# First batch of a fused attention and two-layer MoE kernel: both token parts per third of the gate and value weights

## Chip, cores and metric

The kernel runs on one core of one Trainium2 chip. The metric is device time in microseconds, the median over runs. Engines are named as in the profile: PE (TensorE matmul), PEld (its weight loads), DVE (VectorE), ACT (ScalarE), POOL (GpSimd), SP (SyncE, which here only issues DMAs). ACTq and SPq are the DMA-issuing queues of ACT and SP.

## What is computed

Three stages, cut to what matters:

```python
def _attn_ref(q, k, v, p):                 # q, k, v: 8 x 8 x 576 x 64; p: 8 x 8 x 32 x 64
    p_packed = sm_attn(p, k, v)            # 32 rows per head
    return sm_attn(q, p_packed, p_packed)
def _moe_ref(x, w_gate, w_val, w_out, rms_g):   # 4608 tokens, 512 -> 1536 -> 512
    xn = x / rms * rms_g
    return silu(xn @ w_gate) * (xn @ w_val) @ w_out
def _moe2_ref(x, w_in, w_out, a, b):            # 512 -> 2048 -> 512
    h = x @ w_in
    g = P(h) / (Q(h) + 1e-6)                    # cubic over quadratic
    return g @ w_out
```

The three weights of the first MoE layer arrive as 64-bit floating-point numbers.

## The kernel before

**Batches.** The eight batches of 576 tokens run one after the other through attention and the first MoE layer; the second layer runs at the end over all tokens. A batch's tokens are cut into two parts (`PARTS`): h=0 has 256 of them and h=1 has 320. While batch b is in its MoE layer, attention of batch b+1 is worked in between. Batches 1 to 6 follow an order written out by hand (`BLOCK`). Everything before that, the first batch, is put in order per engine by the framework's list scheduler, which takes the program's order as priority and runs an instruction early where its inputs and buffers are there; the order it finds is fixed before the program runs.

**Precision.** Each matmul is a sum of three fp16 passes over a high and a low half (`PASSES`). So a chain of one output tile has 6 matmuls for the gate or value product and 36 for an output tile of `w_out`.

**Weights of the first layer.** They come in 36 pieces of 128 x 512: eight for each of three thirds `fr` (four of `w_gate`, four of `w_val`), then twelve of `w_out`. For each piece (class `Weights`) the ACT queue issues a DMA of 512 KB into one of three `raw64` buffers (L159). `decode` turns the 64-bit words into fp32 with three DVE instructions (L140, L144, L146) into one of two `raw32` buffers. `split` then makes the two fp16 halves: for gate and value pieces by two fp32 matmuls and an fp16 one on PE (L191, L194, tile `wlo`) and two ACT instructions (L192, L195); for `w_out` by ACT (L115) and DVE (L118).

**M.** The gate and value weights are multiplied with the packed rows of the batch into twelve tiles `mt` (`m_make`: 6 matmuls at L628, then ACT L282 and DVE L283), four to each third. The pool `mt` has 12 buffers. For the first batch `m_make` asks for its weights with `w1.have`, so M0 to M3 pull in the first third's pieces, M4 to M7 the second's, M8 to M11 the third's.

**Gate and value.** For each part h and each of 12 chunks c: a gate chain (L976, 6 matmuls), tanh on ACT (L987), a product on DVE (L991), a value chain (L976), a product on DVE (L994), and the two halves of y by ACT (`y_hi`, L1001) and POOL (`y_lo`, L1006). Four chunks use one third of the weights. The pool `y` has 12 buffers. PSUM has five banks under the tag `m` for all of `wlo`, M, gate, value and output tiles of the first batch.

**Output.** `out1_first` (part h=0 of the first batch) holds all four output tiles in four of those five banks and adds chunk after chunk, so that it can take each piece of `w_out` as it comes (L1042). `out1_slots` (h=1) makes one output tile after the other. `store_x2` writes them out through ACT L1011, DVE L1015 and SP's queue (L1029).

**Slots.** The first batch is cut into 72 slots by the `yield`s of these generators. After each slot `a_step` adds the pieces of attention of batch 1 that `A_PLAN_0` lists for it: `ks`/`kt`, `qs`/`qt`, `vs` are the splits (L115, L118) and transposing DMAs (L358) of k, q, v; `am`...`at` the first softmax (L379 to L436, its transposing DMA on SP); `bm`, `bs`, `bt` the packed rows (L460, L478); `cm`, `cx`, `ce`, `cn`, `ct` the second softmax in three units (matmul L495, DVE L509 to L529, transposing DMA L543); `xm`, `xq`, `xr`, `xt` the attention output and its normalisation into `an`; M0 to M11 the next batch's M. Batch 0's own attention runs before slot 0 in the order `FIRST`. In it and in the plan, `cn` puts the softmax's last product (L529) on DVE and `cN` the same on POOL.

Before the change the slots are: 0 to 23 gate and value of h=0 (the M of a third stands ahead of its first chunk), 24 to 35 `out1_first`, 36 to 59 gate and value of h=1, 60 to 71 `out1_slots` of h=1.

Of the kernel before, what the change touches and what calls it, by code (L numbers as in the profile page):

```python
# [9 lines left out]
F32 = mybir.dt.float32  # L10
F16 = mybir.dt.float16
# [26 lines left out]
def attention_pack_glu_rational_kernel(  # L38
# [22 lines left out]
    KC = DM // 128  # L61
# [213 lines left out]
    def attention(b):  # L275
# [672 lines left out]
    )  # L948

    A_PLAN_0 = (  # L950
# [8 lines left out]
    )  # L959

    FIRST = (
# [3 lines left out]
    )  # L965

# [29 lines left out]
    def y_hi(b, h, c, t):  # L996
        if (b, h) == (B - 1, 1):
            y = yl_p[0].tile([128, 2, PW], F16, name=f"yl{c}")
        else:
            y = y_p.tile([128, 2, PW], F16, tag="y", bufs=YB, name="y")[:, :, 0:t.shape[1]]  # L1000
        act(out=y[:, 0], in_=t, func=AF.Copy)  # L1001
        ys[b, h, c] = y
# [67 lines left out]
        for d in range(KC):  # L1070
            store_x2(b, h, d, pss[d])

    def gv_slots(b, h):
        for c in range(NF1):
            if b == 0 and h == 0 and c % 4 == 0:
                for i in range(c, c + 4):
                    at0[f"M{i}"]()
            ps = gv_mm("g", b, h, c)
            t = gate_tanh(ps)
            gate_mul(t, ps)  # L1080
            yield
            glu_mul(t, gv_mm("v", b, h, c))
            y_hi(b, h, c, t)
            y_lo(b, h, c, t)
            yield
# [51 lines left out]
    for t in (pkz[0], pkz[1], a16, pT):  # L1137
        nc.gpsimd.memset(t, 0.0)
    nc.gpsimd.memset(m_half, -0.5)
    ident = y_p.tile([128, 2, PW], F16, tag="y", bufs=YB, name="ident")  # L1140
    ident = ident.rearrange("p a t -> p (a t)").bitcast(F32)[:, 0:128]
    make_identity(nc, ident)
    nc.gpsimd.dma_start(out=g_raw, in_=rms_g.rearrange("(k p) -> p k", p=128))
    nc.gpsimd.dma_start(out=ab[:, 0:4], in_=pa.rearrange("(o n) -> o n", o=1).to_broadcast([128, 4]))
    nc.gpsimd.dma_start(out=ab[:, 4:6], in_=pb.rearrange("(o n) -> o n", o=1).to_broadcast([128, 2]))
    SH = S_X2 * S_WI2

    def squares(n, name):
        t = y_p.tile([128, 2, PW], F16, tag="y", bufs=YB, name=name).rearrange("p a t -> p (a t)")
        return [t.bitcast(F32)[:, 128 * i:128 * i + 128] for i in range(n)], t[:, 256 * n:256 * n + 128]  # L1150


    diag, minus = squares(2, "diag01")
    diag = diag + squares(2, "diag23")[0]

    def constants():
        nc.vector.tensor_scalar_mul(g_sc, g_raw, S_WGV)
# [20 lines left out]
    def a_step(b, slot):  # L1178
        if b not in plan:
            plan[b] = attention(b + 1)  # L1180
        for at, names in A_PLAN_0:
            if at == slot:
                for nm in names.split():
                    plan[b][nm]()
# [55 lines left out]
            nc.sync.dma_start(out=t, in_=w2_dram[it[:3]])  # L1240

    slot = 0
    for h in range(2):
        for g in (gv_slots(0, h), out1_slots(0, h) if h else out1_first(0, h)):
            for _ in g:
                a_step(0, slot)
                slot += 1
    an.pop(0)
    w2.start()

# [219 lines left out]
```

## Time and profile before

| | us |
|---|---|
| median of 3 runs | 1639.94 (1639.42 to 1644.54) |
| profiled execution, its own time | 1638.45 |
| span in its trace | 1636.3 |
| PE busy | 1538.1 (94%) |
| DVE busy | 1308.2 (80%) |
| first batch ends (PE starts batch 1) | 228.4 after the span's start |

The page gives, among others, the busy share of each engine in 40 equal slices of the span (40.9 us each), the chain of waits that ended last, and groups of instructions. The views by window give busy microseconds of each engine in a stretch, with the granted clock of TensorE as a share of full speed. A group of instructions has its count, busy time, the mean of one in ns, and after the bar the engine's idle time just before them and what ended it.

### The profile page before, as it was taken

How to read it: one execution, taken by the hardware profiler on the slowest of the kernel's cores; microseconds unless marked ns; L12 is line 12 of the kernel's file. 1: busy time of each engine (PE TensorE's matmuls, PEld its weight loads, DVE VectorE, ACT ScalarE, POOL GpSimd, SP SyncE). 2: the span in 40 equal slices, each digit the busy share in tenths (PEclk: the TensorE clock that was granted, in tenths of full speed). 3: DMA queues.
4: the chain of work that ended last, by engine and by line, in shares of the span. 5: the costliest groups of instructions: out<-in, count | busy, mean ns of one | idle time of the engine just before them, and what ended most of it. 6: DMA issues, size and time to landing. Idle time of an engine off the chain costs nothing.

```text
span 1636.3 us, 27117 instructions
## 1 busy us (share of the span) xinstructions
PE 1538.1 (94%) x10158; PEld 901.9 (55%) x10158; DVE 1308.2 (80%) x2201; ACT 937.2 (57%) x1881; POOL 540.5 (33%) x638
## 2 busy tenths in 40 slices
PE   4876899999999998999999999999999999999998
PEld 2424577676767677676776444444444444444443
DVE  5878858678786767867559998989898989898980
ACT  4654547565575655656457756656565656565650
POOL 1200224143342413424233433433343433343430
PEclk9898999999999999999999999999999999999999
DMA  8668427476574746636450101010101010100000
GB/s 204 177 184 201 117 64 191 110 164 145 127 190 93 178 102 149 150 89 139 122 185 15 39 1 52 1 52 1 52 0 52 1 52 1 52 1 26 1 26 26
DMA packets 230899, 144.44 MB, mean 88 GB/s; under 512 B 172272, under 2 KB 208112, under 8 KB 229616
## 3 DMA queue, kind: packets, MB, share of 16 engines
q1 hardware_dynamic: 195600, 91.59, 24.0%
q10 hardware_dynamic: 35072, 51.13, 10.5%
q8 instruction: 79, 1.29, 0.3%
q14 instruction: 52, 0.43, 0.1%
q0 software_dynamic: 96, 0.01, 0.0%
HBM read 82.32 MB, written 27.26 MB: 67 GB/s over the span
## 4 chain that ended last, share of the span: by engine, by line
PE 71%; DVE 16%; DMA 5%; ACT 4%; issue 3%; POOL 1%; ACTq 0%; SPq 0%; DVEq 0%; POOLq 0%
PE h L1315 22%; PE o L1386 21%; PE o L1042 11%; PE gv L976 10%; DVE raw L144 2%; PE mm L856 2%; DVE t L994 2%; DVE t L991 2%; PE xo L814 1%; DVE raw L140 1%; DVE raw L146 1%; PE mm L628 1%; DVE v L699 1%; DMA aT<-a 1%; DMA kT<-x16in 1%
## 5 line engine op out<-in xcount | busy, mean ns | idle before, releaser
L1386 PE MATMUL o<-w2o,g 128*128 128x512 f16 x1728 | 397.3, 380 | 7.1 <-DVE osb L1380 3.8
L1315 PE MATMUL h<-xi,w2i 128*128 128x512 f16 x1728 | 396.3, 379 | 0.0
L976 PE MATMUL gv<-an,mt 128*128 128x256 f16 (+1 forms) x2304 | 302.3, 287 | 19.0 <-DVE t L991 14.3
L1386 PEld LDWEIGHTS <-g 128*128 128x128 f16 x1728 | 169.2, 98 | 214.3 <-issue 7.9
L1042 PE MATMUL o<-y,wo 128*128 128x256 f16 (+1 forms) x2160 | 277.9, 287 | 6.5 <-POOL y L1006 3.2
L1315 PEld LDWEIGHTS <-w2i 128*128 128x128 f16 x1728 | 169.1, 98 | 200.9
L976 PEld LDWEIGHTS <-mt 128*128 128x128 f16 x2304 | 221.2, 98 | 95.3 <-issue 40.0
L1042 PEld LDWEIGHTS <-wo 128*128 128x128 f16 x2304 | 223.3, 98 | 74.1 <-issue 10.2
L1006 POOL TENSOR_TENSOR y<-t,y 128x256 f16<-128x256 f32 (+1 forms) x180 | 139.2, 776 | 315.2 <-ACT y L1001 312.3
L1330 POOL TENSOR_SCALAR w<-ah,cf 128x512 f32<-128x512 f32 x144 | 111.3, 773 | 373.8 <-DVE t L1347 156.4
L1353 POOL TENSOR_TENSOR g<-t,g 128x512 f16<-128x512 f32 x144 | 173.9, 1208 | 99.4 <-issue 71.4
L1327 ACT ACTIVATE ah<-h 128x512 f32<-128x512 f32 x144 | 85.6, 594 | 206.5 <-PE h L1315 206.2
L1345 DVE SCALAR_TENSOR_TENSOR w<-w,r 128x512 f32<-128x512 f32 x144 | 178.8, 1241 | 4.0 <-ACT r L1344 4.0
L1335 DVE TENSOR_TENSOR w<-w,ah 128x512 f32<-128x512 f32 x144 | 135.9, 944 | 0.0
L1333 DVE TENSOR_TENSOR t<-t,h 128x512 f32<-128x512 f32 x144 | 98.3, 683 | 42.6 <-ACT t L1328 42.1
L1328 ACT ACTIVATE t<-h,cf 128x512 f32<-128x512 f32 x144 | 111.5, 774 | 22.8 <-POOL g L1353 22.6
L1015 DVE SCALAR_TENSOR_TENSOR x2e<-o,x2e 128x256 f16<-128x256 f32 (+1 forms) x64 | 29.0, 454 | 106.0 <-ACT x2e L1011 105.9
L1334 DVE SCALAR_TENSOR_TENSOR t<-t,cf,h 128x512 f32<-128x512 f32 x144 | 107.7, 748 | 5.1
L1346 DVE SCALAR_TENSOR_TENSOR t<-t,cf,r 128x512 f32<-128x512 f32 x144 | 107.3, 745 | 0.0
L1001 ACT ACTIVATE y<-t 128x256 f16<-128x256 f32 (+1 forms) x180 | 77.6, 436 | 51.9 <-DVE t L994 51.1
L1347 DVE SCALAR_TENSOR_TENSOR t<-w,t 128x512 f32<-128x512 f32 x144 | 99.6, 692 | 4.9
L1343 ACT ACTIVATE r<-w,one 128x512 f32<-128x512 f32 x144 | 103.5, 719 | 0.0
(192 smaller groups left out, 1795.3 us busy)
## 6 DMA issues: line engine op xcount, KB each, us to landing
raw<-in_moe_w_out_dram ACTq DMA_DIRECT2D x28, 512.0 KB, 4.4
xi<-x2s SPq DMA_DIRECT2D x9, 1024.0 KB, 5.7
raw<-in_v_dram SPq DMA_DIRECT2D x16, 512.0 KB, 4.7
raw<-in_q_dram SPq DMA_DIRECT2D x16, 512.0 KB, 4.9
raw<-in_moe_w_in_dram ACTq DMA_DIRECT2D x16, 512.0 KB, 4.7
out_dram<-osb SPq DMA_DIRECT2D x32, 256.0 KB, 2.5
raw<-in_k_dram SPq DMA_DIRECT2D x14, 512.0 KB, 4.9
raw<-in_moe_w_gate_dram ACTq DMA_DIRECT2D x12, 512.0 KB, 3.8
```

What stands on the lines that cost most here:

```text
L976: nc.tensor.matmul(out=ps, lhsT=mt[b, nm, c // 4, g][:, l, cs], rhs=an[b][:, 2 * r_ + g, cols], start=(n == 0), stop=(n == 5))
L1006: nc.gpsimd.tensor_tensor(out=y[:, 1], in0=t, in1=y[:, 0], op=ALU.subtract)
L1042: nc.tensor.matmul(out=ps, lhsT=wo1[c][:, l, d * 128:(d + 1) * 128], rhs=ys[b, h, c][:, r_, :], start=(c == 0 and n == 0), stop=(c == NF1 ...
L1315: nc.tensor.matmul(out=ps, lhsT=w[:, l, cs], rhs=x2in[j][:, r_, kc, :], start=(n == 0), stop=(n == 3 * KC - 1))
L1328: act(out=t, in_=ps, func=AF.Identity, scale=cf[:, 0:1], bias=cf[:, 7:8])
L1330: nc.gpsimd.tensor_scalar(out=w, in0=ah, scalar1=cf[:, 6:7], scalar2=cf[:, 5:6], op0=ALU.mult, op1=ALU.add)
L1334: stt(out=t, in0=t, scalar=cf[:, 1:2], in1=ps, op0=ALU.add, op1=ALU.mult)
L1335: nc.vector.tensor_tensor(out=w, in0=w, in1=ah, op=ALU.mult)
L1345: stt(out=w, in0=w, scalar=Q1, in1=r0, op0=ALU.add, op1=ALU.mult)
L1346: stt(out=t, in0=t, scalar=cf[:, 2:3], in1=r0, op0=ALU.add, op1=ALU.mult)
L1353: nc.gpsimd.tensor_tensor(out=g[:, 1], in0=t, in1=g[:, 0], op=ALU.subtract)
L1386: nc.tensor.matmul(out=ps, lhsT=gs[j, c][:, l, t * 128:(t + 1) * 128], rhs=w2t["o", 0, c][:, r_, :], start=(c == 0 and n == 0), stop=(c == ...
```

## The change

The first batch no longer finishes part h=0 before it turns to h=1. It takes gate and value of h=0 and then of h=1 with the first third, the same with the second third, then h=0 with the last third, `out1_first` of h=0, h=1 with the last third, and `out1_slots` of h=1:

| slots | before | after |
|---|---|---|
| 0 to 7 | h=0, first third | h=0, first third |
| 8 to 15 | h=0, second third | h=1, first third |
| 16 to 23 | h=0, last third | h=0, second third |
| 24 to 31 | `out1_first` (24 to 35) | h=1, second third |
| 32 to 39 | h=1, first third (36 to 43) | h=0, last third |
| 40 to 51 | h=1, second and last third (44 to 59) | `out1_first` |
| 52 to 59 | | h=1, last third |
| 60 to 71 | `out1_slots`, h=1 | `out1_slots`, h=1 |

With it come four smaller edits. The plan of attention of batch 1 is spread anew: the first softmax and q's split move from slots 11 to 25 and 27 to 30 to slots 16 to 33 and 27 to 31, the packed rows from 25 and 32 to 33 and 37, the second softmax from 34 to 50 to 40 to 51, the attention output from 47 to 61 to 50 to 61, and M0 to M11, which were spread over slots 44 to 63, stand in 60 to 71. `cN` becomes `cn` for unit 0 of batch 0 and unit 2 of batch 1. The y of h=0, chunks 4 to 11, goes into buffers of the pool `mt`. The identity and diagonal matrices go into a buffer of the pool `an` instead of three of the pool `y`.

```diff
     A_PLAN_0 = (
-        (0, "L pl ps"), (2, "ks0 vs0"), (4, "kt0 L"), (6, "pp L"), (8, "ks1 kt1"),
-        (11, "L am0 ax0"), (14, "ae0 as0"),
-        (17, "an0 at0"), (20, "am1 ax1"), (23, "ae1 as1"), (25, "bm0 bs0 bt0 an1 at1"), (26, "vs1"),
-        (27, "L qs0 qt0"), (29, "L"), (30, "qs1 qt1"), (32, "L bm1 bs1 bt1"), (34, "cm0 cx0 ce0"),
-        (37, "cn0 ct0"), (39, "cm1 cx1 ce1"), (42, "cn1 ct1"), (44, "M0"), (45, "cm2 cx2 ce2"),
-        (46, "M1"), (47, "xm0 xq0"), (48, "M2 xr0"), (49, "xt00 xt01"), (50, "M3 cN2 ct2"), (52, "M4"),
-        (53, "xm1 xq1"), (54, "M5 xr1"), (55, "xt10 xt11"), (56, "M6"), (58, "M7 xm2 xq2"), (60, "M8 xr2"),
-        (61, "M9 xt20"), (62, "M10"), (63, "M11"),
+        (0, "L pl ps"), (3, "ks0 vs0"), (6, "kt0 L"), (8, "pp L"), (11, "ks1 kt1"),
+        (16, "L am0 ax0"), (19, "ae0 as0"), (22, "an0 at0"), (25, "am1 ax1"), (27, "L qs0 qt0"), (29, "ae1 as1 L"),
+        (31, "qs1 qt1"), (33, "bm0 bs0 bt0 an1 at1"), (34, "vs1 L"), (37, "bm1 bs1 bt1"), (40, "cm0 cx0 ce0"),
+        (42, "cn0 ct0"), (44, "cm1 cx1 ce1"), (46, "cn1 ct1"), (48, "cm2 cx2 ce2"),
+        (50, "xm0 xq0"), (51, "xr0 cn2 ct2"), (52, "xt00 xt01"),
+        (54, "xm1 xq1"), (55, "xr1"), (56, "xt10 xt11"), (58, "xm2 xq2"), (60, "M0 xr2"),
+        (61, "M1 xt20"), (62, "M2"), (63, "M3"), (64, "M4"), (65, "M5"), (66, "M6"), (67, "M7"), (68, "M8"), (69, "M9"),
+        (70, "M10"), (71, "M11"),
     )
...
+        elif (b, h) == (0, 0) and c >= 4:
+
+            y = mt_p.tile([128, 2, 512], F16, tag="mt", bufs=MTB, name="y0")[:, :, 0:t.shape[1]]
...
-    def gv_slots(b, h):
-        for c in range(NF1):
-            if b == 0 and h == 0 and c % 4 == 0:
+    def gv_first(h, fr):
+
+        b = 0
+        for c in range(4 * fr, 4 * fr + 4):
+            if h == 0 and c % 4 == 0:
                 for i in range(c, c + 4):
                     at0[f"M{i}"]()
             ps = gv_mm("g", b, h, c)
...
-    ident = y_p.tile([128, 2, PW], F16, tag="y", bufs=YB, name="ident")
-    ident = ident.rearrange("p a t -> p (a t)").bitcast(F32)[:, 0:128]
+    squares = an_p.tile([128, 4, S], F16, tag="an", bufs=2, name="squares")
+    squares = squares.rearrange("p a t -> p (a t)").bitcast(F32)
+    ident, *diag = [squares[:, 128 * i:128 * i + 128] for i in range(1 + KC)]
...
-    for h in range(2):
-        for g in (gv_slots(0, h), out1_slots(0, h) if h else out1_first(0, h)):
-            for _ in g:
-                a_step(0, slot)
-                slot += 1
+    parts0 = [gv_first(h, fr) for fr in range(2) for h in range(2)]
+    for _ in itertools.chain(*parts0, gv_first(0, 2), out1_first(0, 0), gv_first(1, 2), out1_slots(0, 1)):
+        a_step(0, slot)
+        slot += 1
```

## Rows read from the trace of the kernel before

**Rows 1.** The page, busy tenths in 40 slices, PE and DVE.

```profile
PE   4876899999999998999999999999999999999998
DVE  5878858678786767867559998989898989898980
```

**Rows 2.** Windows: length, then busy us of PE, PEld, DVE, ACT, POOL, clock, DMA, GB/s.

```profile
67.30:131.00 63.70, 52.60 (x269) 23.53 (x268) 51.31 (x101) 38.40 (x79) 6.08 (x8) 1.00 0.59 167
131.00:178.50 47.50, 30.74 (x306) 23.62 (x305) 39.47 (x84) 18.23 (x40) 4.03 (x5) 0.86 0.91 215
178.50:228.50 50.00, 49.88 (x368) 30.96 (x368) 28.04 (x60) 24.24 (x58) 12.26 (x18) 1.00 0.21 47
67.30:178.50 111.20, 83.34 (x573) 47.15 (x572) 90.78 (x184) 56.63 (x118) 10.11 (x13) 0.94 0.73 188
120.00:140.00 20.00, 16.92 (x134) 10.62 (x134) 17.51 (x34) 11.27 (x27) 3.24 (x4) 1.00 0.54 158
```

**Rows 3.** The chain that ended last, 0 to 320 us: start, length, what.

```profile
50.59 1.38 POOL d L529
...
94.08 1.12 PE wlo L191 x2
...
144.99 8.21 DMA raw<-in_moe_w_out_dram
...
158.92 7.75 DMA qT<-x16in
...
215.40 13.15 PE o L1042 x96
```

**Rows 4.** PE in order of time, 176 to 262 us: start, length, what.

```profile
178.49 4.51 PE L976 MATMUL gv<-an,mt 128*128 128x320 f16 x30 [0.55 <-DVE x2e L1015]
...
183.70 1.80 PE L976 MATMUL gv<-an,mt 128*128 128x320 f16 x12
185.43 0.84 PE L628 MATMUL mm<-wg,pkz 128*64 128x512 f16 x6
...
187.03 1.47 PE L565 MATMUL xo<-pkN,eT 128*128 128x256 f16 x12
188.34 0.98 PE L976 MATMUL gv<-an,mt 128*128 128x320 f16 x6
...
215.34 13.21 PE L1042 MATMUL o<-y,wo 128*128 128x320 f16 x96
228.38 15.88 PE L976 MATMUL gv<-an,mt 128*128 128x256 f16 x144
```

**Rows 5.** Waits, 64 to 180 us: total, times, longest.

```profile
PE pk L460 <- DMA aT<-a: 7.9, 1, 7.9
...
DVE pkz L283 <- ACT pkz L282: 4.2, 1, 4.2
```

**Rows 6.** Groups of DVE, 67.3 to 178.5 us.

```profile
L140 DVE TENSOR_SCALAR raw<-raw 128x512 int32<-128x512 int32 x28 | 13.6, 487 | 6.2 <-PE wlo L191 1.6 <-PE wlo L194 1.5 <-DMA raw<-in_moe_w_val_dram 1.4
L118 DVE SCALAR_TENSOR_TENSOR wo<-raw,wo 128x512 f16<-128x512 f32 x12 | 8.4, 702 | 3.3 <-ACT wo L115 3.2
```

**Rows 7.** Groups of DVE, 178.5 to 228.5 us.

```profile
L994 DVE SCALAR_TENSOR_TENSOR t<-t,gv 128x320 f32<-128x320 f32 x11 | 5.2, 475 | 0.0
...
L542 DVE TENSOR_TENSOR e<-d,e 128x512 f16<-128x512 f32 (+1 forms) x3 | 2.0, 671 | 0.0
...
L529 DVE TENSOR_TENSOR d<-d,s2s 128x512 f32<-128x512 f32 x1 | 0.7, 748 | 0.0
...
L510 DVE TENSOR_TENSOR d<-s,m 64x256 f32<-64x256 f32 x1 | 0.4, 406 | 0.0
```

**Rows 8.** All engines in order of time, 126 to 136 us: DVE beside POOL.

```profile
127.03 0.69 DVE L144 SCALAR_TENSOR_TENSOR raw<-raw,raw 128x512 int32<-128x512 int32 x1
...
132.12 2.56 POOL L1006 TENSOR_TENSOR y<-t,y 128x256 f16<-128x256 f32 x3 [22.95 <-ACT y L1001]
...
134.19 1.04 DVE L144 SCALAR_TENSOR_TENSOR raw<-raw,raw 128x512 int32<-128x512 int32 x1
```

More of the change, by code (lines that the diff above doesn't have):

```diff
@@ L1139, in attention_pack_glu_rational_kernel @@
     nc.gpsimd.memset(m_half, -0.5)
-    ident = y_p.tile([128, 2, PW], F16, tag="y", bufs=YB, name="ident")
-    ident = ident.rearrange("p a t -> p (a t)").bitcast(F32)[:, 0:128]
+    squares = an_p.tile([128, 4, S], F16, tag="an", bufs=2, name="squares")
+    squares = squares.rearrange("p a t -> p (a t)").bitcast(F32)
+    ident, *diag = [squares[:, 128 * i:128 * i + 128] for i in range(1 + KC)]
+    minus = squares.bitcast(F16)[:, 256 * (1 + KC):256 * (1 + KC) + 128]
     make_identity(nc, ident)
@@ L1146, in attention_pack_glu_rational_kernel @@
     SH = S_X2 * S_WI2
[L1148 to L1154, printed above, removed]
     def constants():
```

2 rows, old and new, of the table FIRST are left out of this document.

## The prediction

> **What bounds the kernel now.** I read the page's slices first: over the whole span PE is at 90% or more in nearly every slice; the low ones are all at the start [rows 1]. A saving is therefore to be had only where PE has holes, and the change touches only that region. Next I read the windows. From 67.3 us, where I let the windows begin because batch 0's own attention is done there, to 228.4 us, where PE starts batch 1 [rows 4], there are three stages [rows 2]:
>
> - 67.3 to 131.0, the thirds of the gate and value weights: PE 52.6 of 63.7 us busy, DVE 51.3.
> - 131.0 to 178.5, `out1_first` with the twelve pieces of `w_out`: PE 30.7 of 47.5, DVE 39.5, the granted clock of TensorE 0.86.
> - 178.5 to 228.5, gate, value and output of part h=1 with the next batch's M: PE 49.9 of 50.0, DVE 28.0.
>
> The chain of waits says the same [rows 3]. Up to about 178 us it goes from DVE's decoding to the `wlo` matmuls and back, with DMAs in between (8.2 us for a piece of `w_out`, 7.8 us for q's transpose). Then it is PE alone. So in the first 111.2 us no engine is full (PE 83.3, DVE 90.8) and what sets the time is DVE plus its 20.4 us of idle time [rows 2]; in the last 50 us PE sets it, and DVE rests. The change moves part of the PE-bound work into the DVE-bound stages.
>
> **What leaves the last stage.** A chain of 6 matmuls of h=1 takes 0.865 us: twelve matmuls start at 183.70 and the next row starts at 185.43 [rows 4]. Of the 24 chains of h=1, 20 run in the last stage (120 matmuls; the first of them are the 30 at 178.49 [rows 4]); four were run ahead during `out1_first`. After the change 16 chains stand ahead of `out1_first` and eight behind it. So 20 - 8 = 12 chains leave: 12 x 0.865 = 10.4 us. The attention output `xm0` goes from slot 47 to slot 50, into `out1_first`: 188.34 - 187.03 = 1.3 us [rows 4]. Output (`out1_slots`) and M stay. The last stage becomes 50.0 - 10.4 - 1.3 = 38.3 us. `out1_first` still leaves one of five PSUM banks free, and PE has holes there, so h=1's last third can be run ahead through it as before: none (0 us) to four chains (3.5 us). I take three, 2.6 us, because the situation is nearest to the one that had four. Last stage: 35.7 us (34.8 to 38.3).
>
> **What the first two stages gain in work.** DVE sets them, so I count DVE.
>
> - Gates of h=1: each chunk has two products of 0.475 us [rows 7], 0.95 us. Two chunks were run ahead before; now it is eight, and 1.5 by running ahead: 7.5 more, 7.1 us.
> - The second softmax of batch 1, which in part ran in the last stage, stands wholly in slots 40 to 51. Its seven groups there, from L542 with 2.0 us to L510 with 0.4, sum to 5.8 us [rows 7]; unit 2's product comes back from POOL with at most 0.75. Some of unit 2 will still slip past: I take 5.0 (0 to 6.6).
> - y's low half: POOL works 7.5 times more beside DVE. A decoding instruction takes 0.69 us alone and 1.04 while POOL writes y [rows 8], 0.35 more: 2.6 us (0 if they miss each other; 6.4 if each costs POOL's whole 0.85 us, 2.56 for three [rows 8]).
> - The 16 pieces of gate and value and the 12 of `w_out` (28 decodings, [rows 6]) are neither more nor fewer.
>
> DVE: 90.8 + 7.1 + 5.0 + 2.6 = 105.5 us. PE gains 12 + 3 chains and `xm0`: 83.3 + 13.0 + 1.3 = 97.6 us, so it comes close but DVE stays ahead. ACT (56.6) and POOL (10.1) have room [rows 2]. The lower clock in `out1_first` could return up to 14% of its 30.7 us on PE; as DVE sets that stage, I count nothing.
>
> On POOL there is a rule that speaks against the move. The Trainium skill, page "SBUF — State Buffer", section "Who interferes with whom", says that a DVE instruction with two SBUF inputs and a GpSimd instruction that reads SBUF share a read interface, and the later one blocks fully until the first is done. The trace agrees that they slow each other (0.69 to 1.04 us [rows 8]), but by less than POOL's whole instruction. By the rule at its worst the term is the upper bound, 6.4 us in place of 2.6, and the forecast would be 4 us later.
>
> **How full DVE gets.** This is where I choose. DVE was 81.6% busy in these 111.2 us [rows 2]; the fullest 20 us I found there have 17.51, 88% [rows 2]. Its idle time is partly want of other work: 6.2 us ahead of L140, while a `raw32` buffer is still being read by `wlo` or a DMA is on its way [rows 6]. Gates of h=1 need no weight that is still to come, and can fill such holes. Partly it is a queue standing behind one wait: 4.2 us for the packed rows behind the first softmax's transpose, for which PE waited 7.9 [rows 5], and 3.3 ahead of `wo` behind ACT [rows 6]. Such waits go with the DMA transposes that the plan moves into slots 22 to 33; SP's queue issues them in another order among the loads, and in front of each of them the fixed order of ACT and DVE can stand still again. I take 90%, a little above the best stretch, since the holes that extra work can fill are the larger share: 105.5 / 0.90 = 117.2 us. Bounds: 100% gives 105.5, the old 81.6% gives 129.3.
>
> **Edits that I cost at little or nothing.** `cN0` becomes `cn0`: POOL took 1.38 us on the chain at 50.59 [rows 3], DVE takes 0.75 for the same form [rows 7]; 0 to 0.6 us, I take 0.4. The matrices in a buffer of `an`: the buffer is next wanted at slot 52, long after the last gate or value piece has been split; if that cover were gone, ACT would wait there for a `wlo`, 1.12 us [rows 3]. The y of h=0 in buffers of `mt`: chunks 4 to 7 take fresh ones; M8 to M11 and chunks 8 to 11 take those of thirds whose chains of h=1 are already done, and the next batch's M waits for `out1_first` and the eight chains. Uncovered, this costs a chain (0.87 us) each at most. M now stands one to a slot in 60 to 71, each beside an output piece on a full PE; its cost is unchanged. The attention output must be in `an` by batch 1: before, 41 us lay between the first `xm` at 187.0 and batch 1's start at 228.4, which came without a wait on PE [rows 4]; after, the last stage gives some 36. I cost it at nothing; uncovered, batch 1 would wait for a transposing DMA, 7.8 us by q's [rows 3]. The stores of h=0's output stand on SP's queue ahead of these transposes, as before.
>
> **Sum.** 117.2 + 35.7 = 152.9 us in place of 161.2: 8.3, with `cn0` 8.7. From the profiled execution's 1638.45 (span 1636.3) this is 1629.7; the median shown is 1.5 higher. I forecast 1630.
>
> **Rivals.**
>
> 1. *DVE's idle time stays, 20.4 us* (it is latency, not want of work). 105.5 + 20.4 + 35.7 = 161.6: 1638.5. For it: the order is fixed ahead, and waits on DMA transposes do not care how much work there is. The same time comes out if the scheduler sets h=1's chains behind the weights anyway, so that the change doesn't do what it says. Against: h=1's first third is ahead in priority of the second third's pieces.
> 2. *The extra work packs well*: DVE 98% full, 107.7 + 34.8 = 142.5, less 0.4: 1619. For it: in the stages after batch 0 that are ordered by hand DVE reaches 90% and more in whole slices [rows 1]. Against: the best 20 us here have 88%.
> 3. *Slower: h=1's chains stand in PE's order in front of the `wlo` matmuls.* They come earlier in the program, so a `raw32` buffer is freed a chain later, DVE cannot decode the next piece, and the next 512 KB DMA starts later. If that hits every second one of the 16 gate and value pieces, 8 x 0.865 = 6.9 us of idle time come on top of 20.4: 105.5 + 27.3 + 35.7 = 168.5, 7.3 more less 0.4: 1645. It decides once DVE's idle time there passes 25.3 us, 0.3 us for each piece more than now. For it: the chain of waits alternates between decoding and `wlo` [rows 3], with two buffers only. Against: a chain of h=1 uses PE for 0.87 us while a decoding takes DVE about 1.9 (0.49 for L140 [rows 6], 0.69 for L144 [rows 8], the third taken as the second).
>
> **How the numbers follow.** Forecast (1620 to 1635): 0.48. Rival 2: 0.15. Rival 1: 0.20. Rival 3: 0.17. About 0.3%, 4.9 us, is what a measurement of this kernel can tell from no change: faster 0.48 + 0.15 = 0.63, same 0.20, slower 0.17. The range goes from DVE full (105.5 + 35.7, 1618) to DVE as idle in share as before (129.3 + 35.7, less 0.4: 1642); the tails of rivals 2 and 3 beyond it hold about 0.2.
>
> **What would show it.** The last stage, from the last output matmul of h=0 to PE's first chain of batch 1, should be 35 to 38 us with PE full; if PE has holes there, the attention output or M is late. The two stages before it should be 113 to 121 us from 67 us on, with DVE at 87 to 93% and chains of h=1 between the `wlo` matmuls. If DVE's idle time ahead of L140 is well above 6.2 us, rival 3 holds. If the first two stages come out at about 126 us, rival 1. The forecast is wrong most easily in the 90%: each point is 1.3 us.

## The result, and the profile after

The change makes the kernel slower: median 1651.17 us of 11 runs, against 1641.34 us for the kernel before, ratio 1.0057 with the interval [1.0045, 1.0069]. The forecast was 1630 us. The execution that was profiled took 1643.58 us, the lowest of its eleven, so its trace shows the smaller part of the loss.

In the page's slices of 41 us the first batch is what changes [rows 1]: PE's fourth slice rises from 6 to 8 tenths, and its fifth, 164 to 205 us, falls from 8 to 6.

```profile
PE   4778699989999999999999999999999999999998
DVE  4878747779676767967559998989898989898980
```

The windows of the same stages as in [rows 2] (length, then busy us of PE, PEld, DVE, ACT, POOL, clock, DMA share, GB/s): the thirds up to the first output matmul of h=0, `out1_first`, a hole, the last stage, and the first two together.

```profile
68.50:154.50 86.00, 72.16 (x439) 38.99 (x439) 68.43 (x143) 52.19 (x111) 13.73 (x17) 0.96 0.64 178
154.50:192.00 37.50, 27.79 (x245) 20.52 (x244) 34.48 (x71) 16.60 (x37) 9.35 (x9) 0.91 0.60 167
192.00:198.75 6.75, 0.70 (x7) 0.29 (x4) 2.90 (x8) 0.87 (x4) 0.00 (x0) 0.75 1.11 135
198.75:235.50 36.75, 36.75 (x253) 20.11 (x254) 13.27 (x24) 12.47 (x26) 3.07 (x5) 0.95 0.13 31
68.50:192.00 123.50, 99.95 (x682) 59.51 (x682) 102.91 (x213) 68.79 (x147) 23.08 (x25) 0.94 0.63 174
```

The last stage did what was forecast: 36.75 us, PE busy in all of them. The first two stages hold 102.9 us of DVE's work, but take 123.5 us. Its idle time is 20.6 us, just what it was before (20.4 [rows 2]): 83% full, not 90%. And between them and the last stage lie 6.75 us in which no engine works much and only the DMA engines are full (a share of 1.11). From the first M on PE to batch 1 it is 167.0 us, where it was 161.1.

Who stands in the hole is seen in PE's order of time (start, length, what; in brackets the idle time before and who ended it):

```profile
170.47 1.86 PE L565 MATMUL xo<-pkN,eT 128*128 128x256 f16 x12 [2.71 <-DMA eT<-e]
...
182.09 0.40 PE L565 MATMUL xo<-pkN,eT 128*128 128x256 f16 x1 [2.77 <-DMA eT<-e]
...
198.75 0.64 PE L565 MATMUL xo<-pkN,eT 128*64 128x256 f16 x2 [6.05 <-DMA eT<-e]
199.32 4.81 PE L976 MATMUL gv<-an,mt 128*128 128x320 f16 x24
```

It is the attention output of batch 1 (`xm`), which waits for the transposing DMA of the second softmax. The next row shows what it holds up: 24 matmuls of h=1 that need nothing from it. SP's queue shows the transposes from 100 us on (start, length of the issue, what; a row with x2 runs from the first of two issues to the end of the second):

```profile
101.35 6.13 SPq L358 DMA_TRANSPOSE qT<-x16in  x1
107.52 1.24 SPq L361 DMA_TRANSPOSE qTt<-t16in  x1
...
123.45 4.88 SPq L358 DMA_TRANSPOSE qT<-x16in  x1
...
166.52 12.19 SPq L543 DMA_TRANSPOSE eT<-e  x2
186.88 3.94 SPq L604 DMA_TRANSPOSE an<-n  x2
192.25 1.17 SPq L543 DMA_TRANSPOSE eT<-e  x1
```

q's transposes, which ran in `out1_first` before (one started at 158.92 [rows 3]), now stand among the gate and value pieces. The waits (total, times, longest) name both things, and beside them one that got better: PE waits 1.1 us for `aT`, the transposed first softmax, where it was 7.9 [rows 5].

```profile
PE xo L565 <- DMA eT<-e: 11.5, 3, 6.1
PE wlo L191 <- DVE raw L146: 6.1, 7, 2.0
DVE raw L140 <- DMA raw<-in_moe_w_val_dram: 3.4, 2, 2.6
PE gv L976 <- DVE t L991: 3.2, 1, 3.2
DVE raw L140 <- DMA raw<-in_moe_w_gate_dram: 2.9, 2, 2.5
PE pk L460 <- DMA aT<-a: 1.1, 1, 1.1
```

### The profile page after: what moved, and what is told of

It reads as the page before. It is cut to its first block, busy times and chain, and to the rows that moved or that the text cites. A ratio compares the mean times of both kernels' runs of the same rounds, so it can differ in the third digit from the quotient of the medians.

```text
span 1641.4 us, 27114 instructions
## 1 busy us (share of the span) xinstructions
PE 1540.3 (94%) x10158; PEld 902.1 (55%) x10158; DVE 1310.2 (80%) x2203; ACT 938.0 (57%) x1881; POOL 541.2 (33%) x636
## 4 chain that ended last, share of the span: by engine, by line
PE 73%; DVE 14%; DMA 6%; ACT 3%; issue 2%; POOL 0%; ACTq 0%; SPq 0%; DVEq 0%; POOLq 0%
PE h L1314 22%; PE o L1385 21%; PE o L1045 13%; PE gv L976 11%; PE mm L856 2%; DVE raw L144 2%; DVE t L991 1%; DVE t L994 1%; PE xo L814 1%; DMA aT<-a 1%; DMA eT<-e 1%; DVE raw L140 1%; DVE raw L146 1%; PE mm L628 1%; PE pk L460 1%
## 5 line engine op out<-in xcount | busy, mean ns | idle before, releaser
L1332 DVE TENSOR_TENSOR t<-t,h 128x512 f32<-128x512 f32 x144 | 98.4, 683 | 42.5 <-ACT t L1327 41.9
L987 ACT ACTIVATE t<-gv 128x256 f32<-128x256 f32 (+1 forms) x192 | 77.2, 403 | 47.4 <-PE gv L976 40.3
```

## The experiments

The question is where the forecast saving went, with three candidates: the order of parts itself (chains of h=1 in the way of the weights), q's transposes among the weight pieces, and the second softmax with the attention output in `out1_first`. All kernels are read by the same three stages of their profiled execution: A from the first M on PE to the first output matmul of h=0, B to the end of the last of these, C to batch 1 on PE. In brackets behind a ratio is its 95% interval; two ratios whose intervals overlap much can't be told apart. The runs were on several chips, and each ratio is to runs of the kernel before on the same chip. In e7, e8 and e10 q of batch 1 isn't transposed, and in e11 the second softmax isn't read: these four leave work out and are there for their times alone.

| kernel | A | B | C | sum | ratio to before |
|---|---|---|---|---|---|
| before | 65.4 | 45.0 | 50.7 | 161.1 | 1 |
| after | 86.0 | 37.5 | 43.5 | 167.0 | 1.0057 [1.0045, 1.0069] |
| e1, attention output later | 90.1 | 38.4 | 41.4 | 169.9 | 1.0037 [1.0016, 1.0057] |
| e2, pieces ahead of h=1's chains | 85.3 | 48.7 | 42.6 | 176.6 | 1.0071 [1.0047, 1.0095] |
| e3, new plan, old order of parts | 69.7 | 45.3 | 56.6 | 171.6 | 1.0062 [1.0039, 1.0086] |
| e4, before with `cn` for `cN` | 66.1 | 44.0 | 50.8 | 160.9 | 0.9996 [0.9980, 1.0013] |
| e5, q and what follows late | 90.8 | 30.5 | 36.4 | 157.7 | 0.9976 [0.9960, 0.9992] |
| e6, the same half way | 96.2 | 28.3 | 40.0 | 164.4 | 1.0002 [0.9985, 1.0019] |
| e7, after, q copied | 84.6 | 37.4 | 41.5 | 163.6 | 1.0032 [1.0017, 1.0047] |
| e8, before, q copied | 65.1 | 41.5 | 51.0 | 157.6 | 0.9974 [0.9959, 0.9988] |
| e9, e5 with q held back | 83.8 | 35.3 | 42.5 | 161.6 | 0.9990 [0.9976, 1.0004] |
| e10, e5 with q copied | 85.4 | 30.5 | 36.4 | 152.3 | 0.9946 [0.9924, 0.9968] |
| e11, after, `xo` without `eT` | 91.7 | 34.0 | 39.4 | 165.1 | 1.0028 [1.0012, 1.0044] |
| e12, e5 with q transposed on PE | 87.1 | 31.9 | 37.6 | 156.5 | 0.9958 [0.9942, 0.9975] |

One execution stands behind the stages, all runs behind the ratio; where the two differ, the ratio counts. What follows batch 1's start took 1406 to 1409 us in every one of these profiles, so the rest of the program plays no part. The first M starts at 64.8 to 68.6 us, in the changed kernel 1.2 us later than before.

**e1: the attention output some four slots later.**

```diff
-        (50, "xm0 xq0"), (51, "xr0 cn2 ct2"), (52, "xt00 xt01"),
-        (54, "xm1 xq1"), (55, "xr1"), (56, "xt10 xt11"), (58, "xm2 xq2"), (60, "M0 xr2"),
+        (51, "cn2 ct2"), (54, "xm0 xq0"), (55, "xr0"), (56, "xt00 xt01"),
+        (58, "xm1 xq1"), (59, "xr1"), (60, "M0 xt10 xt11"),
...
```

> The changed kernel, with the attention output of batch 1 (xm, xq, xr, xt of its three units) moved 4 to 5 slots later, behind more of the last third's gate and value chains of h=1; nothing else is changed. Theory W (waits): what the change lost is PE, and behind it ACT and DVE, standing at the xo matmuls for the transposing DMA of the second softmax (2.71, 2.77 and 6.05 us in the changed kernel's trace, the last of them with the other engines idle too). Then 6 to 10 us come back: 1641 to 1645 against 1651 for the changed kernel, as fast as the kernel before (1641) or nearly. Theory A (alternation): the loss lies ahead of out1_first, where chains of h=1 run in one block while decoding and weight DMAs rest; then only the 6 us hole in front of the last stage can come back, and 1645 to 1651 is measured.

The ratio is 1.0037 where it was 1.0057, but the two intervals overlap, and 1645.61 us, the median, is just outside the 1641 to 1645 of theory W. PE's waits for the second softmax's transposes, in the view of waits:

```profile
PE gv L976 <- DVE t L991: 12.1, 2, 8.3
DVE raw L140 <- DMA raw<-in_moe_w_gate_dram: 8.1, 2, 4.1
...
PE xo L565 <- DMA eT<-e: 4.9, 2, 2.5
```

They are 4.9 us in place of 11.5. That they are a part of the loss this run doesn't show by itself; e11 does. And this profile has a new row at its head: PE stood 8.3 us in one piece in stage A, behind DVE, which waited 8.1 us for two gate pieces. It comes back below. The other 3.8 us of that row stand behind `out1_first`, so there is still a hole there, with another cause.

**e2: each piece of the next third decoded ahead of a chain pair of h=1.**

```diff
             y_lo(b, h, c, t)
+            if h == 1 and fr < 2:
+                w1.have(8 * (fr + 1) + 2 * (c % 4) + 2)
             yield
```

> The changed kernel, with the next third's eight weight pieces asked for two by two after each chunk of h=1 (in slots 8 to 15 and 24 to 31), so that decoding and the wlo matmuls have priority ahead of the rest of h=1's chains. Theory A: DVE's idle time from 68.5 to the end of out1_first falls from 20.6 us by 6 to 9, out1_first ends 6 to 9 us earlier, and the time is 1642 to 1645. Theory W: the time stays within 3 us of the changed kernel (1648 to 1654), since the three waits for the transposing DMA remain.

```profile
PE wlo L191 <- DVE raw L146: 12.0, 9, 6.7
...
PE pk L460 <- DMA aT<-a: 8.9, 1, 8.9
DVE raw L140 <- DMA raw<-in_moe_w_val_dram: 6.8, 2, 6.2
```

Stage A is as long as before the edit (85.3 against 86.0), and DVE then waits 6.2 us for a piece that isn't there: it was issued just behind q's first transposing DMA and landed 11.4 us later. So the order of chains and decoding alone does not lengthen stage A, and theory A's 6 to 9 us do not come back. What the order would be worth without the late piece this run can't show.

**e3: the new plan, and the new buffer for the matrices, with the old order of parts.** The y of h=0 is back in the pool `y` (not shown here).

```diff
-    parts0 = [gv_first(h, fr) for fr in range(2) for h in range(2)]
-    for _ in itertools.chain(*parts0, gv_first(0, 2), out1_first(0, 0), gv_first(1, 2), out1_slots(0, 1)):
+    parts0 = [gv_first(0, fr) for fr in range(3)]
+    parts1 = [gv_first(1, fr) for fr in range(3)]
+    for _ in itertools.chain(*parts0, out1_first(0, 0), *parts1, out1_slots(0, 1)):
```

> The changed kernel's plan of attention and its buffer for the matrices, but the parts in the order of the kernel before (h=0 all thirds, out1_first, h=1 all thirds, output), and y of h=0 in the pool y. Theory A: the new order of parts is what costs, so this one is within 3 us of the kernel before (1638 to 1644). Theory W: the plan costs by itself, as the second softmax now falls between h=1's chains; 1645 or more. If the new order gains what was forecast and the plan loses it, this one is slower than the changed kernel (over 1652).

As slow as the change, though no chain of h=1 has moved. It is in theory W's range (1645 or more) with 1651.26 us. Its last stage, in the windows (columns as above):

```profile
180.00:236.57 56.57, 53.40 (x432) 33.10 (x429) 32.70 (x68) 26.48 (x63) 11.50 (x17) 1.00 0.23 50
```

It is 56.6 us, six longer than before, with PE 3.5 us busier [rows 2] and 3.2 us idle: the second softmax, which ran partly ahead of this stage before, now stands wholly in it, and the 3.2 us are `xo` waiting for `eT` here too. Under this plan, then, the old order loses too. From e3 to the changed kernel C falls by 13.1 us and B by 7.8, and A grows by 16.3: what PE gives up in the last stage, stage A takes back most of.

**e4: the product on DVE, alone, in the kernel before.**

```diff
-        (46, "M1"), (47, "xm0 xq0"), (48, "M2 xr0"), (49, "xt00 xt01"), (50, "M3 cN2 ct2"), (52, "M4"),
+        (46, "M1"), (47, "xm0 xq0"), (48, "M2 xr0"), (49, "xt00 xt01"), (50, "M3 cn2 ct2"), (52, "M4"),
```

(and `cN0` likewise.)

> The kernel before with only cN0 and cN2 turned into cn0 and cn2 (two products of the second softmax on DVE in place of POOL). Both theories: 0 to 1 us faster than the kernel before (1640 to 1641); the first xo of batch 0 starts about 1 us earlier after its softmax product.

Nothing that can be told from no change, 0.9996.

**e5 and e6: q's splits and transposes, the second softmax and the attention output late.** e5 puts them behind `out1_first`; e6 has q at slots 40 and 44 and the softmax from 48 on.

```diff
-        (27, "L qs0 qt0"), (29, "ae1 as1 L"), (31, "qs1 qt1"), ...
-        (40, "cm0 cx0 ce0"), (42, "cn0 ct0"), ... (50, "xm0 xq0"), ...
+        (52, "qs0 qt0 L"), (54, "qs1 qt1 L"), (57, "cm0 cx0 ce0"),
+        (59, "cn0 ct0"), (60, "M0 cm1 cx1 ce1"), (61, "M1 cn1 ct1"), (62, "M2 cm2 cx2 ce2"),
+        (63, "M3 xm0 xq0"), (64, "M4 xr0 cn2 ct2"), (65, "M5 xt00 xt01"), (66, "M6 xm1 xq1"), (67, "M7 xr1"),
+        (68, "M8 xt10 xt11"), (69, "M9 xm2 xq2"), (70, "M10 xr2"), (71, "M11 xt20"),
```

> The changed kernel with another plan of attention: q's splits and transposing DMAs go from slots 27 and 31 to 52 and 54, behind out1_first, and all that follows from them (second softmax, attention output) to slots 57 to 71. Theory T (transposes): the transposing DMAs of q delay the weight pieces issued beside them (in the traces so far pieces that were issued beside q's transpose landed 6 to 11 us later, and DVE waited 2.5 to 6.2 us at one piece), and the second softmax takes DVE and ACT in out1_first. Both are gone here, and the last stage has room on DVE and on the DMA queues. The gate and value stage ends some 6 us earlier than in the changed kernel, out1_first lasts 30 to 33 us in place of 37.5, the last stage 42 to 46 in place of 43.5 with its hole: 1634 to 1642. Theory L (latency): the chain from q to the attention output, which now has only the last 20 slots, leaves holes on PE in the last stage, and 1645 or more is measured.

> As the run before, but q's splits and transposing DMAs in out1_first (slots 40 and 44), the second softmax in slots 48 to 57 and the attention output in 56 to 65. Theory T: the gate and value stage gains the 6 us, out1_first loses half of it again, since q's transposes delay pieces of w_out there: 1640 to 1646. Theory L: 1640 to 1645 too, less than the run before, as the chain has more room. If q's transposes are not what delays the pieces, the gate and value stage stays at 85 us or more in both.

e5 turns the change into a small gain, 0.9976. Its 1634.55 us lie in theory T's range, but not by its steps: stage A did not end 6 us earlier, it is 4.8 us longer, and the last stage is 5.6 us shorter than the least that was expected. The windows of its three stages:

```profile
66.20:157.00 90.80, 71.90 (x440) 38.47 (x439) 67.24 (x143) 51.80 (x110) 13.29 (x17) 0.94 0.69 166
157.00:187.50 30.50, 24.64 (x236) 17.73 (x234) 30.37 (x58) 12.42 (x24) 5.85 (x6) 1.00 0.63 195
187.50:223.90 36.40, 35.76 (x265) 20.88 (x263) 20.71 (x45) 18.34 (x42) 4.32 (x8) 1.00 0.29 65
```

`out1_first` is 7.0 us shorter than in the changed kernel, with DVE 30.37 of 30.50 us busy; the hole is gone; and the last stage has not grown by the softmax, since the softmax's matmuls and DVE's share of it fit beside M and the output. 7.0 + 7.1 (C) less the 4.8 that A is longer in this execution is the 9.3 us by which the sums differ. Stage A kept its trouble, because the scheduler ran q's transposes ahead of their slots all the same, at 98.92 and 141.97 us. DVE's rows there, and SP's:

```profile
111.05 0.43 DVE L140 TENSOR_SCALAR raw<-raw 128x512 int32<-128x512 int32 x1 [5.70 <-DMA raw<-in_moe_w_gate_dram]
...
115.11 0.43 DVE L140 TENSOR_SCALAR raw<-raw 128x512 int32<-128x512 int32 x1 [2.18 <-DMA raw<-in_moe_w_gate_dram]
```

```profile
98.92 4.83 SPq L358 DMA_TRANSPOSE qT<-x16in  x1
103.80 1.25 SPq L361 DMA_TRANSPOSE qTt<-t16in  x1
```

The transpose of 98.92 took 14.3 us to land, and the three gate pieces issued beside it 11.5, 10.9 and 11.5 us (4.0 is the median of their group). DVE waited 7.9 us for the first two and PE stood 8.1 us before 117.37: the same long wait as in e1. e6, half way, has the same with 8.5 us and no gain: 1638.39 us, a little under the 1640 that both of its theories start from. By the sign that its expectation names (stage A at 85 us or more in both) q's transposes would not be the cause; but as they were run ahead into stage A in both kernels (at 97.3 and 140.4 us in e6), these two runs do not test that.

**e7 and e8: q of batch 1 copied, not transposed, in the changed kernel and in the kernel before.**

```diff
-            nc.sync.dma_start_transpose(out=xT..., in_=x16...)
-            nc.sync.dma_start_transpose(out=tT..., in_=t16...)
+            nc.sync.dma_start(out=xT..., in_=x16...)          # q of batch 1 only
+            for a_ in range(2):
+                nc.sync.dma_start(out=tT[64 * a_:64 * a_ + 64]..., in_=t16[:, a_]...)
```

> The changed kernel with the transposing DMAs of q of batch 1 replaced by ordinary DMAs of the same bytes from the same source to the same place: q of batch 1 is not transposed. Theory T: it is the transposing kind of the transfer and not its bytes that delays the weight pieces; DVE's waits for pieces in the gate and value stage fall from 6.3 us to under 3, the stage gets 4 to 7 us shorter, 1643 to 1648. If bytes or the number of DMAs matter, or another transpose (k, a) does it, the time stays at 1649 to 1653.

> The kernel before with the same replacement: q of batch 1 is copied, not transposed. There q's transposes lie in out1_first. Theory T: out1_first gets 4 to 8 us shorter (PE waited 4.5 us for q's transpose, and w_out pieces landed up to 8.2 us after their issue), 1633 to 1637. If the pieces are late for another reason, 1639 or more.

Both times are in theory T's ranges (1643.29 and 1633.92 us). The ratio falls by 0.0025 in the changed kernel (4.1 us, give or take 3) and by 0.0026 in the kernel before (4.3 us, give or take 2.4). In e8 the profile has it in B, 41.5 us in place of 45.0. In e7's profile the other expectations fail: DVE's waits in stage A were to fall under 3 us, and are

```profile
DVE raw L140 <- DMA raw<-in_moe_w_val_dram: 3.2, 2, 1.6
...
DVE raw L140 <- DMA raw<-in_moe_w_gate_dram: 2.1, 2, 1.3
```

5.3 us where they were 6.3, and A is 1.4 us shorter, not 4 to 7. The slowest piece beside q's first copy took 7.1 us, the slowest beside its first transpose in the changed kernel's profile 6.2. But that profile is of the fastest of eleven runs, and has no 8 us wait in it; what e7 saves is in the medians. By them q's transposes cost about four microseconds in either place: the change did not make them dearer. Where the changed kernel pays them is seen in the next runs.

**e9, e10 and e12: what keeps stage A long in e5.** In e9 a small DVE copy ties q's split to the last chunk of h=0, so that no transpose can run ahead. In e10 q is copied as in e7. In e12 q is transposed by matmuls, as k of batch 0 is.

```diff
+            if nm == "q" and b == 1:                                                       # e9
+                nc.vector.tensor_copy(out=x16[:, 0, 0, 0, 0:16], in_=ys[0, 0, 11][:, 0, 0:16])
+                nc.vector.tensor_copy(out=t16[:, 0, 0, 0:16], in_=ys[0, 0, 11][0:TAIL, 0, 0:16])
...
-        (52, "qs0 qt0 L"), (54, "qs1 qt1 L"), (57, "cm0 cx0 ce0"),                          # e12
+        (40, "qf0 L"), (44, "qf1 L"), (57, "cm0 cx0 ce0"),
```

> The kernel of e5_q_late (new order of parts; q's splits, second softmax and attention output in slots 52 to 71), and the split of q of batch 1 is tied by one small DVE copy per buffer to y of the last chunk of part h=0, so that no transpose of q can be issued before that chunk is done. In e5_q_late the scheduler had run them ahead: a transposing DMA of q issued at 98.92 us landed 14.3 us later, a weight piece beside it 11.2 us after its issue, DVE waited 7.9 us for gate pieces and PE stood 8.1 us before 117.4. Theory (q's transposes delay the weight pieces): the stage from the first M to the first output matmul falls from 90.8 to 80-85 us, no gate or value piece lands later than 7 us after its issue, the 8 us stall is gone; out1_first takes 33-37 in place of 30.5 us, because the transposes now stand beside the pieces of w_out; time 1626 to 1634 on a chip where the kernel before has 1638. Rival (the pieces are late by the order of decoding and wlo matmuls whatever SP does): the stage stays at 88-91 us and the time is 1636 or more.

> The kernel of e5_q_late with q of batch 1 copied by ordinary DMAs of the same bytes in place of the transposing ones (q of batch 1 is left untransposed, so its attention is computed from the wrong layout); places in the plan unchanged, the copies are still issued ahead among the gate and value pieces. Theory (it is the transposing that delays the pieces, not the place on SP's queue): stage from first M to first output matmul 82-86 us in place of 90.8, pieces land within 7 us, time 1628-1631 where the kernel before has 1638. Rival (the queue or the splits ahead of them delay): stage 88-91 us, time 1634 and more.

> The kernel of e5_q_late with q of batch 1 transposed on PE (matmuls against the identity, as k of batch 0 is in this kernel) in slots 40 and 44, in place of splitting it and transposing it by DMA; nothing is left out. The rows of k of batch 0 give the price: 8 matmuls of 0.42 us and two of 0.29 on PE, 4.0 us a group, 8.0 for both; ACT and DVE do about what the split cost them. Theory (q's transposing DMAs are what keeps the gate and value stage from its forecast length): from the first M to the first output matmul 85 to 90 us, where e5_q_late had 90.8 and the kernel with copied q 85.4; no gate or value piece later than 7 us; out1_first 30 to 33, last stage 36; first M to batch 1 152 to 158 us, time 1628 to 1633 where the kernel before has 1638. Rival (PE becomes the bound of that stage: 72 of 85 us busy already): the whole 8.0 us shows, first M to batch 1 160 us, time 1636 to 1639.

Stage A falls from 90.8 to 83.8, 85.4 and 87.1 us, and the 8 us wait of PE is in none of the three. DVE's waits for gate and value pieces are 7.9 and 1.9 us in e5; in e10 they are

```profile
DVE raw L140 <- DMA raw<-in_moe_w_val_dram: 1.5, 1, 1.5
...
DVE raw L140 <- DMA raw<-in_moe_w_gate_dram: 0.6, 1, 0.6
```

So q's transposes make the pieces late: in e1, e5, e6 and e11 the three gate pieces beside the first of them landed after 9.8 to 12.0 us; beside the same bytes, copied from the same place on SP's queue, no gate or value piece took over 7.1 (e7, e10), and with no q in the stage none over 5.5 (e9, e12). In the changed kernel's own profile they took 6.2 at most, so it doesn't happen in every execution. In all four late cases the load of batch 1's k stood just ahead on SP's queue, and pieces beside e5's second transpose landed in 4.1 to 5.5 us; whether that load has a part in it was not tested. In e10 the load stood there too, and the copy did no such harm. In e9 the transposes then stand in `out1_first`, and PE meets them there:

```profile
179.24 0.34 PE L498 MATMUL s<-pkz,qT 128*128 128x64 f16 x3 [5.52 <-DMA qT<-x16in]
```

B becomes 35.3 us (33 to 37 was expected), and C 42.5, which was not: PE waits another 2.7 us there for q's second transpose and has the second softmax's matmuls to do behind it. So e9's time, 1637.61 us, is outside the 1626 to 1634 that its theory gave; in these profiles holding q back gains 7.0 us in A and loses 10.9 behind it.

e10 reaches the length that was forecast, 152.3 us where 152.9 was. Its ratio, 0.9946, is 0.0030 lower than e5's (give or take 0.0027). Its windows:

```profile
67.34:152.73 85.39, 72.74 (x441) 38.37 (x440) 67.11 (x143) 51.56 (x110) 13.25 (x17) 0.96 0.63 177
...
183.27:219.68 36.41, 35.77 (x266) 20.91 (x264) 20.74 (x45) 18.30 (x42) 4.32 (x8) 1.00 0.29 65
67.34:183.27 115.93, 97.41 (x674) 56.09 (x673) 97.52 (x200) 64.00 (x134) 19.09 (x22) 0.97 0.64 182
```

But it comes by another way: DVE is 84% full in the first two stages (97.5 of 115.9), not 90%, and of the 7.6 us by which they are shorter than in the changed kernel 5.4 are DVE's work that is not in them any more (102.9 - 97.5).

e12 does all of the work and has the lowest ratio of the kernels that do, 0.9958 of the kernel before with 1633.12 us, though its interval overlaps that of e5. PE's price for q is less than I took from batch 0's k, where I had added up the lengths of single instructions (0.42 us), which overlap in a row:

```profile
158.46 0.65 PE L329 MATMUL kTf<-squares,raw 128*128 128x128 f32 x4
...
163.93 0.34 PE L337 MATMUL kTf<-squares,rawt 64*128 64x64 f32 x2 [0.17 <-DVE qT L283]
```

Two of the first and one of the second for each half of q: 3.3 us in all in place of 8.0, and they run in `out1_first`, where PE has room. The Trainium skill, page "VectorE: DVE Perf Modes", section "Rules for kernel authors", says to transpose 128x128 blocks on TensorE where a PSUM destination is all right and by DMA otherwise; the run fits that, with 0.16 us a block in a row of four, but its time can't be told from e5's.

**e11: the attention output matmuls read a weight tile in place of `eT`.**

```diff
             eT = st.pop(("eT", u))
+            if b == 1:
+                eT = wgv['g', 0, 0].rearrange('p a t -> p (a t)').rearrange('p (e t) -> p e t', t=128)
```

> The changed kernel, but the attention output matmuls of batch 1 read a weight tile in place of the transposed second softmax (so that output of batch 1 is wrong); the softmax and its transposing DMAs are still worked. It takes away the waits of PE for those DMAs alone: 11.5 us in the profile of the changed kernel, 6.05 of them in the hole in front of the last stage. Theory (these waits cost time of their own): the hole of 6 us is gone, out1_first ends at 186-190 us, time 5 to 8 us below the changed kernel's, ratio to before 0.998-1.003. Rival (DVE would have set the same end, waits covered): out1_first ends at 192 us as in the changed kernel, time within 2 us of its 1651, ratio 1.005-1.007.

The ratio is 0.0029 lower (give or take 0.0020), 4.8 us by the 1640 us of the whole, a little under the 5 to 8 expected. The 6 us wait for `eT` is gone, and batch 1 starts 39.4 us after B's end in place of 43.5. The hole is not gone whole. PE's first chains behind `out1_first` now wait for the last output tiles of h=0 to be worked off by DVE:

```profile
195.47 5.91 PE L978 MATMUL gv<-an,mt 128*128 128x320 f16 x30 [3.09 <-DVE x2e L1020]
```

In the changed kernel DVE had done that at 194.5, so of its 6.05 us wait, from 192.7 to 198.75, some 4 were the transposing DMA's alone. That B ends at 191.8, where the rival put it, is due to A, which was 5.7 us longer in this execution; B itself is 3.5 shorter. As nothing holds `xm` back here, the scheduler also set it earlier in PE's order (the last of it at 176 us, where it was at 204), so the run takes away the waits and the place together. So the waits for `eT` cost time of their own. e5, which takes the second softmax's work out of `out1_first` as well, gains 0.0081; that its larger part is that work in the stage that DVE sets is argued.

## Why the prediction was wrong

By its own steps, for the profiled execution:

- *Last stage, 35.7 us.* It took 36.75 with PE full, +1.1. Right.
- *DVE's work in the first two stages, 105.5 us.* It was 102.9, 2.6 less. Right. The 2.6 us for POOL's y did not show where I had looked for them: the 28 decodings of L144 took 0.71 us each, as before. They show in the splits of k and q, of the kernel before first and of the changed one below:

```profile
L118 DVE SCALAR_TENSOR_TENSOR x16in<-raw,x16in 128x256 f16<-128x256 f32 x12 | 4.4, 416 | 0.1
...
L118 DVE SCALAR_TENSOR_TENSOR x16in<-raw,x16in 128x256 f16<-128x256 f32 x12 | 6.8, 593 | 1.6 <-ACT x16in L115 1.6
```

  With those of the small tiles, six that started while POOL wrote y took 0.56 to 1.02 us, where one takes 0.41 alone: 2.6 us in all. That this is the sum I had is luck, since it was worked out for other instructions. The rule of the Trainium skill (page "SBUF — State Buffer", section "Who interferes with whom") that was weighed there is not borne out at its worst; by it DVE would have had 3.8 us more than forecast. In kind it is: a split that was already running when POOL's instruction started took 0.41 to 0.43 us, as alone.
- *How full DVE gets, 90%.* This step failed. It was 83.3%: 123.5 us in place of 117.2, +6.3 (by 90% the 102.9 us would have taken 114.3, so the step itself is 9.2 us short, and 2.9 came back by the work). I had written that DVE's waits go with the transposing DMAs that the plan moves, and then let extra work fill them. Extra work did come in, and new waits with it. DVE's idle time ahead of L140 did not shrink but has other causes now, 6.3 of 7.6 us for gate and value pieces on their way, where a `raw32` buffer still in use was half of it [rows 6]. And the gates of h=1, which were to fill holes, bring their own: ahead of their first product DVE waited 3.8 us for ACT's tanh. The decoding and the products, over 68.5 to 192.0 us:

```profile
L144 DVE SCALAR_TENSOR_TENSOR raw<-raw,raw 128x512 int32<-128x512 int32 x28 | 19.8, 710 | 0.3
...
L140 DVE TENSOR_SCALAR raw<-raw 128x512 int32<-128x512 int32 x29 | 12.7, 441 | 7.6 <-DMA raw<-in_moe_w_val_dram 3.4 <-DMA raw<-in_moe_w_gate_dram 2.9 <-PE wlo L191 0.9
...
L991 DVE SCALAR_TENSOR_TENSOR t<-t,gv 128x320 f32<-128x320 f32 x9 | 4.3, 481 | 3.8 <-ACT t L987 3.8
```

- *The attention output, costed at nothing.* This step failed too. I asked whether it would be done by batch 1, 36 us on, and it was. But in a fixed order a matmul has an earlier due time: that of whatever stands behind it on its engine. `xm2` stands in front of 24 matmuls, four chains, of h=1, so its 6.05 us wait was PE's, and 6.75 us went by, of which some 4 would have been saved without it (e11). I had moved the second softmax and the output into `out1_first` in the sum, 5.0 and 1.3 us of work, and not the transposing DMA between them.
- *`cn0`, 0.4 us.* No difference in e4.

152.9 + 1.1 + 6.3 + 6.75 = 167.0 us, what was measured; from 161.1 that is 5.9 us more. The first M came 1.2 us later, and what follows batch 1's start took 2.0 less: 1638.45 + 5.9 + 1.2 - 2.0 = 1643.6, the time of the execution. The other 7.6 us up to the median are not in this profile. In the profiles of e1, e5, e6 and e11, which have the same order of parts and run a transpose of q among the gate and value pieces too, PE stands 8.1 to 8.5 us at one place behind a late gate piece. That most runs of the changed kernel do the same, and are slower for it, is argued, not shown; this part of the cause stays open.

Of the rivals, the first named the idle time to the microsecond (20.4 forecast as staying, 20.6 measured), but not the hole, and so gave 1638.5. The closeness is in part luck: the waits that make it up are not the old ones. The third had the sign and the wrong mechanism: idle time behind `wlo` went down from 3.1 us [rows 6] to 0.9, and e2, which gives the weights the way, is no faster. Of the signs that the prediction named beforehand, holes on PE behind `out1_first` if the attention output is late is the one that came.

What the order of parts together with the late plan is worth is seen where q does not stand in its way: e10 against e8, both with q copied, 0.9946 against 0.9974, some 4.6 us, give or take 4.3. DVE is 79% busy in stage A even then (67.1 of 85.4 us in e10). Of the 18.3 us idle, 5.9 stand ahead of L140, 4.9 ahead of the low halves of M (L283), behind ACT, and 3.7 ahead of the products of h=1, behind ACT's tanh. What would shorten them stays open; more than two `raw32` buffers were not tried.

## What to carry to other kernels

In a fixed order a step is due when the next thing behind it on its engine is, not when its result is used: ask of every moved matmul that reads a transposed or loaded tile how long its DMA takes and what queues behind it. When work is moved into a stage because an engine has idle time there, look at what ends those idle times; where it is DMAs in flight and the plan moves more DMAs in, count the idle time as staying. And ask what the work that is moved in waits for itself. Work that is not urgent, and has DMAs in its middle, belongs beside the stage that another engine fills: there it was nearly free (e5's last stage, 36.4 us with the softmax in it against 36.75 without).

## What the runs showed of the hardware

A transposing DMA can be a bad neighbour. q's 512 KB land 6.6 us after their issue as an ordinary copy (median of two, e10), and 9.0 (the changed kernel) to 11.9 us (e5) as a transposing one, and three weight pieces of 512 KB beside one took 10.9 to 11.5 us in place of 4.0 (e5). Beside the other one in e5 they took 4.1 to 5.5 us, and beside the first one in the changed kernel's profile 5.9 to 6.2; what decides between these is not shown. The page "Advanced Engine Details and Errata" of the Trainium skill, section "X-Bar Transpose (TRN2)", says that transposing DMAs are as fast as regular ones on this chip; these runs differ, and by the medians the kernel is some 4 us longer for the two halves of q (e7, e8). Alone on the queues the effect was not measured.

POOL's work can slow DVE's: a split of 128x256 that started while POOL wrote y took 0.56 to 1.02 us, alone 0.41 to 0.43 (the changed kernel).

The granted clock of TensorE was 0.82 on average in e2's `out1_first` (PE 30.4 of 48.7 us busy, with an 8.9 us wait in it) and 1.00 in e5's and e10's, where PE was 24.6 and 24.7 of 30.5 us busy without long waits. I had not counted a gain from it, and as DVE sets that stage in e5 and e10 none is shown.
